# A squared-ReLU attention and GeGLU block: transposing DMAs by row chunk, stores as operations of their own, loads spread out, and the first batch in two query halves

## The chip, the cores and the metric

The kernel runs on one core of one Trainium2 chip. The metric is the device time of one execution in microseconds, the median of several runs.

## The reference

For 8 batches, 12 heads, 448 positions and a head width of 64, attention with a squared ReLU in place of a softmax; the heads are then laid side by side to rows of 768, and a gated feed-forward block with 1536 hidden columns follows:

```python
scores = scale * np.matmul(q, k.transpose(0, 1, 3, 2))     # scale = 1/8
attn = np.maximum(scores, 0.0) ** 2 / S
x = np.matmul(attn, v)            # to (B * S, H * D) = (3584, 768)
g = x @ w_gate
gelu = 0.5 * g * (1.0 + erf(g * inv_sqrt2))
out = gelu * (x @ w_val) @ w_out  # (3584, 768), float32
```

All inputs are float32; the kernel computes in bfloat16 and accumulates in float32.

## The kernel before

**Tiles.** TensorE is used as four 64x64 quarters. Every matmul (line 151, `mm`) names its row half and its column half; rows 0 and rows 1 are planned as two streams, PE0 and PE1. Positions are dealt so that partition p holds positions 7p to 7p+6 (`SC` = 7 chunks of `P` = 64).

**Work of a batch.** There are 21 score units (`add_scores`): each is a block of transposed scores, 128 x 896, of which ScalarE makes the ReLU (`rl`, line 339) and VectorE the square (`attnT`, line 345). `add_values` multiplies them with v for a pair of heads and VectorE scales the result into `xT` (line 394). When all six pairs are there, `add_gate_value` computes the 12 column blocks `fc` of gate (g = 0) and value (g = 1), 6 contraction steps each; ScalarE makes the gelu, VectorE the product, `uT`. `add_out` computes one tile of 128 rows in two column halves, ScalarE copies it to `osb` (line 484), and SP stores it (line 489).

**q and k must be transposed** (tile `qkT`) for the scores. For batches 0 to 2 (`EARLY` = 3) TensorE does it (`add_transposes`, line 290) with VectorE copying the result (line 296). For batches 3 to 7 `add_dma_transposes` does it: VectorE reorders q and k into `qkr` in seven copies (line 240), and one transposing DMA, issued by SP, writes all of `qkT` (line 248).

**Order.** `work` is a list of due times: attention of batch b+1 is spread under gates, values and outputs of batch b; batch 0's attention stands ahead of everything. `run_plan` then places all operations on a model clock. PE0 and GpSimd keep the given order; PE1, ScalarE, VectorE and SP take from a pool what is ready first. The result is one fixed order per engine, and each engine runs its order without overtaking. PSUM has two buffers for scores (`SB`) and a ring of four for everything else (`FB`): a ring buffer is free when VectorE or ScalarE has emptied it.

**Loads** are all issued by GpSimd in one order, and land in it: batch 0 in head groups, then the weight chunks `wg`/`wv` 0 to 5 with batch 1's heads between them, the four `wo` chunks, and then what `add_gate_value` adds as it goes: batch 2 as a whole (q, k, v), later batches in three parts per tensor, q and k three batches ahead and v two. A tile's two buffers (`qkv` pool) are reused every second batch.

**Stores** are issued inside the emission of ScalarE's copy of the second column half. They stand in SP's order at the place where that copy was planned; SP's order also holds the transposing DMAs.

Of the kernel before, what the change touches and what calls it, by code (L numbers as in the profile page):

```python
# [85 lines left out]
def kernel(  # L86
# [17 lines left out]
    P = 64  # L104
# [15 lines left out]
    EARLY = 3  # L120
# [13 lines left out]
    opool = ctx.enter_context(tc.tile_pool(name="opool", bufs=3))  # L134
# [95 lines left out]
    def add_dma_transposes(b):  # L230

        box = {}

        wait = Op("IDLE", 8.0, lambda: None, [head_op[b, pr, i] for pr in range(NPAIR) for i in range(2)])
        IDLE.append(wait)

        def emit_copy(c):
            if not box:
                box[0] = lpool.tile([128, SC, H, D], bf16, name="qkr", tag="qkr")
            nc.vector.tensor_copy(  # L240
                box[0][:, c], qk16[b].rearrange("p (h c d) -> p c h d", c=SC, d=D)[:, c])

        copies = [Op("DVE", 0.4, lambda c=c: emit_copy(c),
                     [wait, tr_op.get(b - 1)], lag=0.1, prio=3)
                  for c in range(SC)]
        DVE.extend(copies)
        r_op[b] = copies
        tr_op[b] = Op("SP", 7.0, lambda: nc.sync.dma_start_transpose(
            qkT_tile(b)[:, :, :], box[0].rearrange("p c h d -> p (c h d)")),
            [*copies, last_s.get(b - 2)], lag=6.0)  # L250
        SP.append(tr_op[b])
# [10 lines left out]
    def both(at, ops):  # L262

        for lo, hi in ops:
            lower.append((at, lo))
            pairs.append(("with", lo, hi))
# [13 lines left out]
    def add_transposes(at, b, m):  # L280
# [30 lines left out]
        both(at, zip(*ops))  # L311

    def add_scores(at, b, u):


        m, w = divmod(u, SC)
        tail = w == VC - 1
        prs = (2 * m, 2 * m + 1) if tail else (2 * m + (w > VC - 1),)
        cl = w if w < VC else w - VC
        box = {}  # L320

        def emit(j, pr):
            if not box:
                box[0] = psS.tile([128, 2, 512], f32, name="sp", tag="S")
            sp = box[0]
            t = qkT_tile(b).rearrange("d (c r) x -> d r c x", c=SC)[HALF[j], pr]
            for i in range(2):
                if tail:
                    n0 = (pr % 2) * S // 2
                    qs = t[:, :, i * P // 2:(i + 1) * P // 2]  # L330
                    mm(sp[HALF[i], j, n0:n0 + S // 2].rearrange("k (c p) -> k c p", c=SC),
                       t[:, VC - 1, HALF[1]], qs, j, i, True, True)
                else:
                    mm(sp[HALF[i], j, 0:S].rearrange("k (c p) -> k c p", c=SC),
                       t[:, cl + i * VC, HALF[1]], t[:, :, HALF[0]], j, i, True, True)

        def emit_relu():
            rl = box[1] = rpool.tile([128, 2, S], bf16, name="rl", tag="rl")
            nc.scalar.activation(rl[:, :, :], box[0][:, :, 0:S], AF.Relu)  # L339

        def emit_sq():
            a = apool.tile([128, 2, S], bf16, name="attnT", tag="attnT")
            for pr in prs:
                att[b, pr, VC - 1 if tail else cl] = a
            nc.vector.tensor_tensor(a[:, :, :], box[1][:, :, :], box[1][:, :, :], op=ALU.mult)  # L345

        if b < EARLY:
            have = [t_op[b, m, 0], t_op[b, m, 1]]
        else:
            have = [tr_op[b]]  # L350
        have = [*have, *units[-SB:1 - SB]]
        ops = [[Op(f"PE{j}", 0.095 if tail else 0.189, lambda j=j, pr=pr: emit(j, pr), have, lag=0.24)
                for pr in prs] for j in range(2)]
        last_s[b] = ops[1][-1]
        relu = Op("ACT", 0.92, emit_relu, [ops[0][-1], ops[1][-1], *sq_list[-4:-3]], lag=0.06, prio=2)
        n_a = len(sq_list)
        sq = Op("DVE", 0.64, emit_sq, [relu, *att_free[n_a - 12:n_a - 11]] if n_a >= 12 else [relu],
                lag=0.1, prio=2)
        units.append(relu)
        sq_list.append(sq)  # L360
        att_free.append(None)
        for pr in prs:
            sq_op.setdefault((b, pr), []).append((sq, n_a))
        ACT.append(relu)
        DVE.append(sq)
        both(at, zip(*ops))
# [3 lines left out]
    def add_values(at, b, pr):  # L370
        box = {}

        def emit(i, w):
            if pr == 0 and i == 0 and w == 0:
                xT[b] = xpool.tile([128, KC, S], bf16, name="xT", tag="xT")
            if not box:
                box[0] = psF.tile([128, 512], f32, name="ff", tag="F")
            if i == 1 and w == VC - 1:
                wait_lower(box)
            for j in range(2):  # L380
                o = box[0][HALF[j], 0:S]
                a = att[b, pr, w][HALF[i], j, :]
                if w < VC - 1:
                    ins = mm(o, v16[b][HALF[i], 2 * pr + j, w + i, :], a, i, j,
                       i == 0 and w == 0, i == 1 and w == VC - 2)
                else:
                    ins = mm(o.rearrange("d (c p) -> d c p", c=SC)[:, :, i * P // 2:(i + 1) * P // 2],
                       v16[b][HALF[i], 2 * pr + j, (1 - i) * (VC - 1), :],
                       a[:, (pr % 2) * S // 2:(pr % 2 + 1) * S // 2].rearrange(
                           "k (c p) -> k c p", c=SC), i, j, False, False)  # L390
            box[1] = ins

        def emit_copy():
            nc.vector.tensor_scalar_mul(xT[b][:, pr, :], box[0][:, 0:S], scalar1=out_scale)  # L394

        sqs = sq_op[b, pr]
        have = [*(s for s, _ in sqs), head_op[b, pr, 2], head_op[b, pr, 3]]
        order = ([0, 1, 2, 3], [3, 0, 1, 2])
        ops = [[Op(f"PE{i}", 0.189 if w < VC - 1 else 0.095, lambda i=i, w=w: emit(i, w),
# [5 lines left out]
        x_op[b, pr] = Op("DVE", 0.63, emit_copy, [o_op[b, pr]], lag=0.1, prio=1)  # L405
        DVE.append(x_op[b, pr])
        ring.append(x_op[b, pr])
        then(at, 0.0, *ops, x_op[b, pr])
# [5 lines left out]
    def add_gate_value(at, b, fc, g):  # L414

        i, o = divmod(fc * 128, WCH)
# [3 lines left out]
        def emit(r, dc):  # L420
# [4 lines left out]
            for j in range(2):  # L425
                ins = mm(box[0][HALF[j], 0:S], w[HALF[r], dc, o + P * j:o + P * (j + 1)],
                         xT[b][HALF[r], dc, :], r, j, r == 0 and dc == 0, r == 1 and dc == KC - 1)
            box[1] = ins

        def emit_gelu():  # L430
            gel[b, fc] = gpool.tile([128, S], bf16, name="gel", tag="gel")
            nc.scalar.activation(gel[b, fc][:, :], box[0][:, 0:S], AF.Gelu)  # L432

        def emit_mult():
            if fc == 0:
                uT[b] = upool.tile([128, FC, S], bf16, name="uT", tag="uT")
            nc.vector.tensor_tensor(uT[b][:, fc, :], gel.pop((b, fc))[:, :],  # L437
                                    box[0][:, 0:S], op=ALU.mult)

        ops = [[Op(f"PE{r}", GS, lambda r=r, dc=dc: emit(r, dc),  # L440
                   [w12_op[i][g], x_op[b, dc], *(ring_dep() if r == 0 and dc == 0 else ())], lag=0.24)
                for dc in range(KC)] for r in range(2)]
        if g == 0:
            done = gel_op[b, fc] = Op("ACT", 0.55, emit_gelu, [ops[1][-1]], lag=0.06, prio=0)
            ACT.append(done)
        else:
            done = u_op[b, fc] = Op("DVE", 0.63, emit_mult, [gel_op[b, fc], ops[1][-1]],
                                    lag=0.1, prio=0)
            DVE.append(done)
            if EARLY <= b + 2 < B and fc == 0:  # L450
                add_dma_transposes(b + 2)
            if b == 0 and fc == 0:
                load_heads(2, 0, H)
            elif b + 2 < B and b and 6 <= fc < 9:
                load_v(b + 2, 4 * (fc - 6), 4 * (fc - 5), [done])
            if b + 3 < B and fc < 6:
                h0 = 4 * (fc % 3)
                load_qk(b + 3, fc // 3, h0, h0 + 4, [done])
        ring.append(done)
        then(at, GS, *ops, done)  # L460

    def add_out(at, t, g):
# [17 lines left out]
        def emit_copy():  # L480
# [4 lines left out]
            if g < NG - 1:  # L485
                return
            for j, (b, c) in enumerate(chunks):
                rows = out[b * S:(b + 1) * S, :].rearrange("(p c) d -> c p d", c=SC)
                nc.sync.dma_start(rows[c], ob[HALF[j], :])  # L489

        ops = [[Op(f"PE{r}", RS, lambda r=r, fc=fc: emit(r, fc),
                   [wo_op[fc // WOG], *(u_op[b, fc] for b, _ in chunks),
# [4 lines left out]
        ACT.append(cp)  # L497
        then(at, RS, *ops, cp)
# [5 lines left out]
    load_heads(1, 0, 4)  # L504
    load_w12(1)
    load_w12(2)
    load_heads(1, 4, 8)
    load_w12(3)
    load_heads(1, 8, 12)
    load_w12(4)  # L510
    load_w12(5)
    for i in range(FC // WOG):
        load_wo(i)

# [6 lines left out]
    for b in range(B):  # L521
        starts.append(at)
        for fc in range(FC):
# [11 lines left out]
    for b in range(B):  # L535
        if b == 0:
            lo, hi = -60.0, -12.0
        elif b == 1:
            lo, hi = -8.0, starts[1] - LEAD
# [6 lines left out]
        for pr in range(NPAIR):  # L546
            u = SC * (pr // 2) + (VC - 1, SC - 1)[pr % 2]
            work.append((lo + u * step + max(4.5, (3.2 if b == 0 else 2.5) * step), 2, add_values, (b, pr)))
# [5 lines left out]
    for at, _, fn, args in work:  # L554
        fn(at, *args)
# [75 lines left out]
```

## Time and profile before

| | us |
|---|---|
| runs | 454.03, 455.63, 452.81 (median 454.03) |
| profiled execution, whole time | 456.05 |
| its span in the profile | 454.2 |

The page divides the span into 40 slices of 11.4 us, gives each engine's busy time, the chain of work that ended last, and groups of instructions by line: engine, what it writes and reads, shapes, count, then busy time, mean ns of one, and the engine's idle time before them with what ended it. Some groups around the change:

```profile
L339 ACT ACTIVATE rl<-sp 128x896 bf16<-128x896 f32 x168 | 152.6, 920 | 119.7 <-PE sp L151 102.2
...
L432 ACT ACTIVATE gel<-ff 128x448 bf16<-128x448 f32 x96 | 52.2, 544 | 57.4 <-PE ff L151 55.8
...
L290 PE MATMUL ff<-ident,qk 64*64 64x64 bf16 x504 | 15.2, 213 | 7.4 <-DMA qk<-in_q_dram 3.3
```

The DMA issues (what, queue, count, size of one, median time from issue to landing):

```profile
wv<-in_moe_w_val_dram POOLq DMA_DIRECT2D x6, 384.0 KB, 11.3
wo<-in_moe_w_out_dram POOLq DMA_DIRECT2D x4, 576.0 KB, 15.7
v<-in_v_dram POOLq DMA_DIRECT2D x2, 384.0 KB, 22.0
```

Sizes are of the bfloat16 side; HBM is read in float32.

### The profile page before, as it was taken

The page shows a single profiled execution, that of the slowest core. Times are in us where ns is not written, and L with a number is a line of the kernel's source. Part 1 is how long each engine was busy: PE and PEld are TensorE (multiplying, and loading weights), DVE is VectorE, ACT ScalarE, POOL GpSimd, SP SyncE. Part 2 cuts the span into 40 slices and gives each one's busy share as a digit, 9 for nine tenths or more (in the row PEclk, how much of TensorE's full clock was granted, in tenths as well). Part 3 has the DMA queues.
Part 4 walks back from the last instruction along what each step waited for, and adds up shares of the span by engine and source line. Part 5 has one row for each costly group of instructions (what it writes and reads, how often), then busy time and mean ns, then how long its engine had stood idle before and what let it go on. Part 6 is the DMA issues. An engine that isn't in the chain of part 4 may idle for free.

```text
span 454.2 us, 20046 instructions
## 1 busy us (share of the span) xinstructions
PE 429.1 (94%) x9360; PEld 364.6 (80%) x9360; DVE 207.7 (46%) x366; ACT 226.0 (50%) x322; POOL 70.7 (16%) x114
## 2 busy tenths in 40 slices
PE   5779999999799999999999799999999999999995
PEld 2546987878699778987799578999999878987895
DVE  1794555464453356545553255535543355312200
ACT  1785554545355555555555455555555655422121
POOL 9545421041301500060002000030000000000000
PEclk8595999999999999999999899999999999999998
DMA  7999999389938960497009800291002200120024
GB/s 100 187 198 198 204 208 202 74 107 156 162 55 136 222 100 3 81 197 146 3 3 153 183 1 3 57 207 39 3 3 73 72 4 3 38 73 3 3 72 105
DMA packets 68659, 43.56 MB, mean 96 GB/s; under 512 B 29664, under 2 KB 64992, under 8 KB 68576
## 3 DMA queue, kind: packets, MB, share of 16 engines
q0 software_dynamic: 37056, 24.39, 37.9%
q1 hardware_dynamic: 31520, 17.90, 18.7%
q8 instruction: 73, 1.20, 1.1%
q14 instruction: 10, 0.08, 0.0%
HBM read 48.76 MB, written 11.01 MB: 132 GB/s over the span
## 4 chain that ended last, share of the span: by engine, by line
PE 87%; DMA 4%; ACT 3%; POOL 2%; issue 2%; DVE 2%; SPq 0%; ACTq 0%; POOLq 0%
PE ff L151 78%; PE sp L151 8%; DMA out_dram<-osb 2%; ACT rl L339 2%; DMA qk<-in_k_dram 2%; PE ff L290 1%; POOL qk L198 1%; POOL v L211 1%; DVE qkT L296 1%; DVE attnT L345 1%; ACT osb L484 0%; SPq L489 0%; DVE xT L394 0%; DVE uT L437 0%; POOL ident masks.py:199 0%
## 5 line engine op out<-in xcount | busy, mean ns | idle before, releaser
L151 PE MATMUL ff<-xT,wg 64*64 64x448 bf16 x2304 | 230.5, 353 | 4.0 <-ACT osb L484 3.3
L151 PE MATMUL ff<-xT,wv 64*64 64x448 bf16 x2304 | 229.7, 351 | 0.4 <-issue 0.4
L339 ACT ACTIVATE rl<-sp 128x896 bf16<-128x896 f32 x168 | 152.6, 920 | 119.7 <-PE sp L151 102.2
L151 PEld LDWEIGHTS <-wg 64*64 64x64 bf16 x2304 | 133.4, 108 | 25.6 <-issue 8.4
L151 PE MATMUL ff<-wo,uT 64*64 64x384 bf16 x2688 | 149.9, 323 | 0.3 <-DVE uT L437 0.2
L151 PEld LDWEIGHTS <-wv 64*64 64x64 bf16 x2304 | 134.0, 108 | 18.1 <-issue 2.2
L345 DVE TENSOR_TENSOR attnT<-rl 128x896 bf16<-128x896 bf16 x168 | 104.0, 623 | 92.2 <-ACT rl L339 91.4
L151 PEld LDWEIGHTS <-uT 64*64 64x64 bf16 x2688 | 124.4, 107 | 5.8 <-DVE uT L437 0.6
L151 PE MATMUL sp<-qkT 64*64 64x448 bf16 (+1 forms) x768 | 115.7, 350 | 7.0 <-ACT rl L339 4.3
L437 DVE TENSOR_TENSOR uT<-gel,ff 128x448 bf16<-128x448 bf16 x96 | 59.5, 620 | 75.8 <-PE ff L151 71.3
L151 PE MATMUL ff<-attnT,v 64*64 64x448 bf16 (+1 forms) x768 | 91.6, 339 | 0.0
L432 ACT ACTIVATE gel<-ff 128x448 bf16<-128x448 f32 x96 | 52.2, 544 | 57.4 <-PE ff L151 55.8
L151 PEld LDWEIGHTS <-qkT 64*64 64x64 bf16 x768 | 48.1, 112 | 20.1 <-issue 11.5
L211 POOL DMA_DIRECT2D v<-in_v_dram x46 | 28.8, 649 | 166.1 <-PE sp L151 87.8
L151 PEld LDWEIGHTS <-v 64*64 64x64 bf16 x768 | 48.4, 110 | 3.8 <-issue 0.3
L484 ACT COPY osb<-ff 128x384 f32<-128x384 f32 x56 | 26.8, 479 | 46.1 <-PE ff L151 37.4
L394 DVE TENSOR_SCALAR xT<-ff 128x448 bf16<-128x448 f32 x48 | 29.9, 624 | 39.2 <-PE ff L151 33.4
L290 PE MATMUL ff<-ident,qk 64*64 64x64 bf16 x504 | 15.2, 213 | 7.4 <-DMA qk<-in_q_dram 3.3
L198 POOL DMA_DIRECT2D qk<-in_q_dram x23 | 14.8, 653 | 41.0 <-DVE qkr L240 21.3
L290 PEld LDWEIGHTS <-qk 64*64 64x64 bf16 x504 | 14.3, 127 | 8.1 <-DMA qk<-in_q_dram 3.8
L296 DVE COPY qkT<-ff 128x896 bf16<-128x896 bf16 x18 | 10.9, 623 | 14.3 <-PE ff L290 12.1
L198 POOL DMA_DIRECT2D qk<-in_k_dram x23 | 14.6, 644 | 14.4 <-DMA qk<-in_k_dram 4.3
(17 smaller groups left out, 33.3 us busy)
## 6 DMA issues: line engine op xcount, KB each, us to landing
out_dram<-osb SPq DMA_DIRECT2D x56, 192.0 KB, 4.0
v<-in_v_dram POOLq DMA_DIRECT2D x40, 128.0 KB, 7.1
qk<-in_q_dram POOLq DMA_DIRECT2D x20, 224.0 KB, 9.8
qk<-in_k_dram POOLq DMA_DIRECT2D x20, 224.0 KB, 10.8
wg<-in_moe_w_gate_dram POOLq DMA_DIRECT2D x6, 384.0 KB, 11.0
wv<-in_moe_w_val_dram POOLq DMA_DIRECT2D x6, 384.0 KB, 11.3
wo<-in_moe_w_out_dram POOLq DMA_DIRECT2D x4, 576.0 KB, 15.7
v<-in_v_dram POOLq DMA_DIRECT2D x2, 384.0 KB, 22.0
```

The source lines that it names most:

```text
L151: return nc.tensor.matmul(o, lhsT, rhs, start=start, stop=stop, tile_position=(P * row, P * col))
L198: op = load(4 * (h1 - h0) * S * D, lambda: nc.gpsimd.dma_start(tile_of().rearrange("p (h x) -> p h x", h=H)[:, h0:h1, :], src[b, h0:h1].re ...
L211: nc.gpsimd.dma_start(v16[b][HALF[i], h0:h1, :, :], v[b, h0:h1].rearrange("h (p c) d -> p h c d", c=SC)[:, :, c0:c0 + VC, :])
L290: nc.tensor.transpose(t[HALF[j], pr, c * P:(c + 1) * P], src[HALF[i], 2 * (2 * m + pr) + j, c, :], ident[HALF[i], HALF[i]], tile_position= ...
L296: nc.vector.tensor_copy(dst[:, 2 * m:2 * m + 2, :, HALF[i]], box[i].rearrange("d r (c p) -> d r c p", c=SC))
L339: nc.scalar.activation(rl[:, :, :], box[0][:, :, 0:S], AF.Relu)
L345: nc.vector.tensor_tensor(a[:, :, :], box[1][:, :, :], box[1][:, :, :], op=ALU.mult)
L394: nc.vector.tensor_scalar_mul(xT[b][:, pr, :], box[0][:, 0:S], scalar1=out_scale)
L432: nc.scalar.activation(gel[b, fc][:, :], box[0][:, 0:S], AF.Gelu)
L437: nc.vector.tensor_tensor(uT[b][:, fc, :], gel.pop((b, fc))[:, :], box[0][:, 0:S], op=ALU.mult)
L484: nc.scalar.copy(ob[:, cols], box[0][:, 0:OGS])
```

## The change

- `EARLY` is 2: batch 2 is transposed by DMA too. Its `add_dma_transposes` is called just before its first score unit is added.
- The transposing DMA of a batch is seven DMAs, one per row chunk c, each behind its own `qkr` copy. Scores of the batch depend on all seven.
- The planned wait between the landing of q and k and the copies is 2 us instead of 8.
- Each store is an operation of its own in SP's pool, with the lowest priority number; `osb` has four buffers instead of three.
- Loads: chunks 1 and 2 of `wg`/`wv` stand before batch 1's heads, q and k of batch 2 before `wo`, v of batch 2 after it. From batch 3 on, q and k are loaded two batches ahead instead of three: one part behind each of the first six products of batch b, then v behind the next three.
- Batch 0 is worked through in two halves `hq` of its queries (32 of the 64 positions of each chunk): score units of 448, 448, 448 and 224 columns per two pairs, values, and gates and values of the first `NA` = 6 column blocks, all at half width. Scores of the second half are due from 6 us ahead of the first gates on. Blocks 6 to 11 are computed at full width.
- Batch 1's attention is due from 5.0 instead of -8.0; a few planned costs are written as formulas of the width.

```diff
-    EARLY = 3
+    NA = 6
+    EARLY = 2
...
-    opool = ctx.enter_context(tc.tile_pool(name="opool", bufs=3))
+    opool = ctx.enter_context(tc.tile_pool(name="opool", bufs=4))
...
-        wait = Op("IDLE", 8.0, lambda: None, [head_op[b, pr, i] for pr in range(NPAIR) for i in range(2)])
+        wait = Op("IDLE", 2.0, lambda: None, [head_op[b, pr, i] for pr in range(NPAIR) for i in range(2)])
...
-        tr_op[b] = Op("SP", 7.0, lambda: nc.sync.dma_start_transpose(
-            qkT_tile(b)[:, :, :], box[0].rearrange("p c h d -> p (c h d)")),
-            [*copies, last_s.get(b - 2)], lag=6.0)
-        SP.append(tr_op[b])
+        tr_op[b] = [Op("SP", 1.1, lambda c=c: nc.sync.dma_start_transpose(
+            qkT_tile(b).rearrange("d (c r) x -> d c r x", c=SC)[:, c],
+            box[0][:, c].rearrange("p h d -> p (h d)")),
+            [copies[c], last_s.get(b - 2)], lag=6.0) for c in range(SC)]
+        SP.extend(tr_op[b])
...
+    def pieces(b, u):
+        m, w = divmod(u, SC if b else 2 * 4)
+        x, y = 2 * m, 2 * m + 1
+        mid = VC - 1
+        if b:
...
+        n = S // 4
+        return [[(x, 0, 0, 2 * n), (x, 1, 2 * n, 2 * n)],
+                [(x, 2, 0, 2 * n), (x, mid, 2 * n, n), (y, mid, 3 * n, n)],
+                [(y, 0, 0, 2 * n), (y, 1, 2 * n, 2 * n)],
+                [(y, 2, 0, 2 * n)]][w % 4]
...
-            have = [tr_op[b]]
+            have = tr_op[b]
...
-    def add_gate_value(at, b, fc, g):
+    def add_gate_value(at, b, fc, g, hq=None):
+        p0, QP = (0, P) if hq is None else (hq * P // 2, P // 2)
+        N = SC * QP
...
-            if EARLY <= b + 2 < B and fc == 0:
-                add_dma_transposes(b + 2)
-            if b == 0 and fc == 0:
-                load_heads(2, 0, H)
-            elif b + 2 < B and b and 6 <= fc < 9:
-                load_v(b + 2, 4 * (fc - 6), 4 * (fc - 5), [done])
-            if b + 3 < B and fc < 6:
+            if b + 2 < B and b and fc < 9:
                 h0 = 4 * (fc % 3)
-                load_qk(b + 3, fc // 3, h0, h0 + 4, [done])
+                if fc < 6:
+                    load_qk(b + 2, fc // 3, h0, h0 + 4, [done])
+                else:
+                    load_v(b + 2, h0, h0 + 4, [done])
+                if fc == 5:
+                    add_dma_transposes(b + 2)
...
-            if g < NG - 1:
-                return
-            for j, (b, c) in enumerate(chunks):
-                rows = out[b * S:(b + 1) * S, :].rearrange("(p c) d -> c p d", c=SC)
-                nc.sync.dma_start(rows[c], ob[HALF[j], :])
+        def emit_store(j):
+            b, c = chunks[j]
+            rows = out[b * S:(b + 1) * S, :].rearrange("(p c) d -> c p d", c=SC)
+            nc.sync.dma_start(rows[c], osb[t][HALF[j], :])
...
+        if g == NG - 1:
+            SP.extend(Op("SP", 0.6, lambda j=j: emit_store(j), [cp], prio=-1) for j in range(2))
...
     load_w12(0)
-    load_heads(1, 0, 4)
     load_w12(1)
     load_w12(2)
+    load_heads(1, 0, 4)
+    load_w12(3)
     load_heads(1, 4, 8)
-    load_w12(3)
+    load_w12(4)
     load_heads(1, 8, 12)
-    load_w12(4)
     load_w12(5)
+    load_qk(2, 0, 0, H)
+    load_qk(2, 1, 0, H)
     for i in range(FC // WOG):
         load_wo(i)
+    load_v(2, 0, H)
...
+        for hq in range(0 if b else 2):
+            for fc in range(NA):
+                for g in range(2):
+                    work.append((at, 5, add_gate_value, (b, fc, g, hq)))
+                    at += G / 2
+        for fc in range(0 if b else NA, FC):
...
+    for hq in range(2):
+        lo, step = ((-60, 2.0), (-6.0, 0.9))[hq]
+        for u in range(4 * NPAIR // 2):
+            work.append((lo + u * step, 3, add_scores, (0, u, hq)))
```

## The prediction

> **What bounds the kernel now.** I read the page from the top: which engine is busy, at what clock, in which slices.
>
> ```profile
> PE 429.1 (94%) x9360; PEld 364.6 (80%) x9360; DVE 207.7 (46%) x366; ACT 226.0 (50%) x322; POOL 70.7 (16%) x114
> ...
> PE   5779999999799999999999799999999999999995
> ...
> PEclk8595999999999999999999899999999999999998
> DMA  7999999389938960497009800291002200120024
> ```
>
> TensorE is the bound, except at the start: its clock is down in the first four slices, while the DMA row is full. "Busy" says little here, since a matmul that uses a quarter of the array counts as busy. So I count work. In the windows 410 to 420 us (220 matmuls of 64x448) and 430 to 440 us (254 of 64x384) TensorE is packed: 0.102 ns for each streamed column, edges included. I take 0.104, so a 448-column matmul is 47 ns of work. The page's counts give (4608 + 672 + 672) x 448 + 2688 x 384 + 504 x 64 columns (the scores and values, 768 each, count as 672, a quarter of them being half wide): 388.6 us of work. The other 65.6 us of the 454.2 us span are lost. Counting the same way by window, the loss is 31.8 us before 50 us, 3.5 to 80, 8.4 to 130, 4.5 to 250, 4.4 in 250 to 260, 6.4 to 440 and 6.4 in the tail.
>
> The windows show the three kinds of loss:
>
> ```profile
> 25.00:50.00 25.00, 21.64 (x392) 16.15 (x392) 16.68 (x29) 16.45 (x21) 13.15 (x19) 0.80 1.42 198
> ...
> 110.00:120.00 10.00, 7.11 (x174) 5.17 (x174) 4.28 (x8) 3.08 (x6) 1.31 (x3) 1.00 1.35 166
> ...
> 250.00:260.00 10.00, 7.42 (x130) 4.88 (x125) 2.21 (x4) 4.63 (x7) 0.08 (x1) 0.83 0.89 204
> ```
>
> Columns: length, busy time and count of TensorE, weight loads, VectorE, ScalarE, GpSimd, clock, DMA. Where a packed window of 10 us has 220 matmuls, 250 to 260 has 130, and part of it at half clock. The chain of waits names the causes (start, length, what), and the SP queue's timeline shows what stands behind the second:
>
> ```profile
> 115.20 2.54 issue
> ...
> 246.53 6.21 DMA out_dram<-osb
> ```
> ```profile
> 94.97 50.58 SPq L248 DMA_TRANSPOSE qkT<-qkr  x2
> ...
> 238.84 7.01 SPq L248 DMA_TRANSPOSE qkT<-qkr  x1
> 245.94 10.05 SPq L489 DMA_DIRECT2D out_dram<-osb  x8
> ```
>
> Stores wait in SP's queue behind one transposing DMA of 7 us. ScalarE's copy then waits 4.0 us for a free `osb`, TensorE 2.6 us for ScalarE.
>
> The DMA view settles my forecast; first 104 to 108 us, where the transposing DMA of batch 3 meets loads, then 140 to 144 us, where one runs alone:
>
> ```profile
> q0 software_dynamic: 713, 0.57, 89.8%
> q1 hardware_dynamic: 712, 0.18, 34.6%
> ...
> qkT<-qkr SPq DMA_TRANSPOSE x1, 27.3
> ```
> ```profile
> q1 hardware_dynamic: 3134, 0.80, 147.9%
> ...
> qkT<-qkr SPq DMA_TRANSPOSE x1, 8.7
> ```
>
> Packets go one for one. A transpose is 5376 packets of 256 bytes, 336 for each of 16 engines: 6.9 us alone. Beside loads it gets one packet per load packet, and took 27.3 us to land instead of 8.7.
>
> [...]
>
> **The change, part by part.** Positions are work issued before an instruction, in the order in which the built program issues.
>
> *First batch in halves.* The first gate matmul moves from 10.3 us of work (reached at 37.6 us) to 6.7. Its ScalarE chain: 10.5 relu units per half at 0.82 us back to back (nine in 7.40 us); the heads land as before (the last q and k near 17 us). About 18 relu units stand before the first gelu, so gates begin near 28 us. The next block is batch 1's first transposes at 9.2 us of work. With two more gate/value chunks loaded ahead of them (four loads, 2.0 us apart in the trace), these heads land at about 33.7 us (25.7 in the trace). Before stood at 9.2 at 34 us too, but still had its first gates to wait for and ran at half clock through the page's fourth slice (34 to 45 us)[...]. I take it to be 3 us of work ahead at 50 us. Cost: 312 more matmuls net. [...] VectorE and ScalarE get 15 and 9 more, shorter, instructions; both are idle half the time. All this lies ahead of the wait named next, which hides it; uncovered it would be 0 to 3 us.
>
> *Loads moved.* q and k of batch 2 (672 KB each) go ahead of the four `wo` loads, v of batch 2 behind. The last `wv` lands at 53.7 us (issued 42.36, median 11.3); q and k took 3.35 us each (k is 3.3 us behind q). So k of batch 2 lands at 60.4 us. VectorE, in order, now has a `qkr` copy of batch 2 at 26 us of work, waiting for that k: behind it stand gate multiplies, hence PSUM banks, so TensorE is at 30 or less at 60.4 us (before: 27.4). Whatever the halves win beyond that is lost here.
>
> *Batch 2 by DMA.* 168 TensorE transposes go: 1.1 us of work, and the loss around them. Each window of ten us with 56 of them loses about 1.5 us more than its neighbours; 112 lie after the place below. In their stead seven `qkr` copies (0.354 us each, VectorE has room) and seven transposing DMAs. The four stores of batch 0 stand behind them on SP, which is no loss: they come later anyway. The DMAs start at 61 to 66 us, with `wo` and v of batch 2 (192 packets per engine, to 76.2 us without company) in flight. One for one, 192 of the 336 go by while the loads last; the rest follow. If nothing is lost in sharing, all is done at 76.2 + 6.9 + 1 = 84. In the one meeting that the trace has (the same 192 load packets, 10.8 us alone), loads plus transpose took 23.3 us, so the transpose added 12.5: 76.2 + 12.5 + 1 = 90. I take 87.5. The first score matmul of batch 2 waits for all seven and stands at 44.2 us of work. TensorE would be there at 60.6 + 14.2/0.94 = 76 us (`wo`, delayed by 96 transpose packets, is in by 76). So it waits some 11 us, everything behind it in its one order too: outputs of batch 0, gates of batch 1. Before passed 44.2 at 79.4. [...]
>
> *Stores and transposes later.* Seven short issues in place of one of 7 us, stores on their own, a fourth `osb`: the loss in 250 to 260 us (4.2 above the base), 150 to 160 (1.4) and 300 to 310 (1.0) goes. Could it cost? Each store still waits in line behind transposes, but those stand a third of a batch earlier, 13 us of work ahead of their use against 9.8 us of landing. Next in line would be that margin. Loads of q and k one per gate column, not two batches ahead: 4 to 5 us to landing against about 5 us in the order; a late one stops VectorE for a microsecond. I add 1.5 us for both (0 to 4).
>
> **Sum.** Remaining work at the wait is 387.5 - 44.2 = 343.3 us, 7.7 of it in the last 14.2 us, which stay. The rest runs with the loss that 130 to 250 and 260 to 440 us show without the store waits, (10.9 - 2.4) in 300 us, 2.8%: 345.2. So 87.5 + 2.6 + 345.2 + 14.2 + 1.5 = 451.0 of span, against 454.2: 3.2 less. The profiled execution took 456.05 in all, 1.85 beyond its span; the median is 454.03. I forecast 454.0 - 3.2 = 451 (rounded), and 447 to 455 for 84 to 91 us. Less than 1% (4.5 us) I count as no change that a measurement of this kernel can tell.
>
> **Rivals.** *The transpose isn't late*: sharing is cheaper, or the wait shorter than I see. TensorE passes 44.2 at 76 to 83 us: 436 to 446, faster. For: the alternating packets at 104 to 108 us add up without loss. Against: the 27.3 us. *The transpose is very late*: at 100 to 104 us the two queues crept. If the sharing goes that way throughout, at 80 ns per transpose packet, 192 of them put the loads' end to 92 and the rest to 96: 460, slower. It is slower than before from a landing at about 91 us, by over 1% from 95. *The store waits stay*: SP still takes its queue in order; then 6.6 us come back: 456 to 458.
>
> **Chances.** Forecast mechanism 0.60, transpose in time 0.18, very late 0.12, store waits stay 0.10. Faster by over 1%: 0.18 and nearly 0.4 of the first, 0.41. Slower: 0.12 and a little of the last, 0.13. Same: 0.46. The range 439 to 458 leaves out half of the second case and most of the third.
>
> **What would show it.** Right: gates from about 28 us; transposing DMAs issued at 61 to 66 us and the last landing at 84 to 91; TensorE idle at the first `sp` matmul of batch 2 with the DMA as its releaser, and half clock after; no wait of ScalarE on `out_dram` in the middle. Wrong: no idle time between 75 and 90 us, a landing outside 84 to 91, or a wait in each batch on `qkr` copies or transposes.

## The result, and the profile after

| | before | after |
|---|---|---|
| runs | 454.03, 455.63, 452.81, 455.41 | 460.44, 460.9, 461.96, 458.95 |
| median | 454.72 | 460.67 |
| profiled execution, whole time | 456.05 | 460.44 |
| its span | 454.2 | 458.7 |

The ratio is 1.0134 (95% interval 1.0085 to 1.0183): slower, by about 6 us, where 3 less were forecast. (Medians and ratios here are taken over undisturbed runs alone, and a ratio can differ a little from the quotient of two medians.)

The page of the kernel after, busy shares and rows of 40 slices (11.5 us each):

```profile
PE 430.5 (94%) x9672; PEld 382.4 (83%) x9672; DVE 207.5 (45%) x382; ACT 226.7 (49%) x331; POOL 70.7 (15%) x114
...
PE   6896579879999999999999999999999999999995
...
PEclk8559899979999999999999999999999999999998
DMA  8999999929635490729374881762092200120023
```

After slice 9 little is lost. The damage is in slices 4 to 9, where the row of before had 9s: TensorE at 6, 5, 7 tenths with the DMA row at 9. The chain of waits of after (start, length, what) names it; these are all its lines over 1.4 us between 35 and 95 us that are no work of TensorE:

```profile
39.22 2.41 issue
...
45.39 2.43 issue
...
51.34 2.69 issue
...
58.48 1.46 issue
...
63.95 1.92 issue
...
88.60 5.93 DMA qkT<-qkr
```

Two things, then. Five gaps of about 2 us, one every 6 us, that no semaphore explains ("issue"). And the wait on the transposes of batch 2, forecast for 76 to 87.5 us. The chain counts it from the issue of the last transposing DMA; TensorE itself waits less, as its own waits between 75 and 100 us show (what, on what: total us, times, longest):

```profile
PE sp L152 <- DMA qkT<-qkr: 3.0, 1, 3.0
PE ff L152 <- issue: 1.7, 1, 1.7
```

It stands at 88.7 to 90.4 us in a sixth gap, works for 1.3 us, and waits for the transposes from 91.7 to 94.7.

The same counting of work as in the prediction (0.104 ns per column) gives, over time, what TensorE had done in after less what it had done in before:

| at us | 45 | 50 | 55 | 60 | 70 | 85 | 95 | 105 | 250 | 270 | 430 |
|---|---|---|---|---|---|---|---|---|---|---|---|
| us of work | +1.6 | -1.1 | -4.5 | -6.5 | -10.7 | -8.6 | -13.5 | -15.5 | -10.4 | -6.2 | -5.2 |

At 70 us after is 10.7 us behind. Seven more go between 85 and 105: at the sixth gap, at the transposes and in the half clock behind them (94.3 to 101.1 us). Some 10 come back: 4 between 105 and 120 us, where before has a stall of its own, and 4 at 250 to 270, where the store waits are gone.

**The five gaps.** The windows of 38 to 68 us, in before and in after (length; busy and count of TensorE, weight loads, VectorE, ScalarE, GpSimd; clock; DMA share, over 1 where packets overlap in time; GB/s):

```profile
38.00:68.00 30.00, 29.88 (x634) 26.52 (x632) 16.71 (x29) 16.27 (x22) 11.59 (x16) 0.89 1.30 204
```
```profile
38.00:68.00 30.00, 19.18 (x600) 17.06 (x599) 11.33 (x25) 11.73 (x19) 9.55 (x13) 0.93 1.30 204
```

Look at the counts. Before executes 634 matmuls in these 30 us and after 600: nearly the same number, but after's are narrow, so it needs only 19 us for them and stands still for 11. So the limit counts instructions, not columns (e1 below). Numbering all instructions of TensorE (a weight load and a matmul each count one), the gaps stand at number 1473, 1729, 1985, 2241 and 2497: exactly 256 apart. The sixth, at 3521, is on the same grid. The DMA view of after, 38 to 68 us, has a queue that the prediction passed over (packets, MB, share):

```profile
q0 software_dynamic: 7817, 6.01, 128.9%
q8 instruction: 5, 0.08, 1.0%
```

Five packets of 16384 bytes, at 39.19, 45.55, 51.58, 57.66 and 63.53 us; each of the five gaps ends 2.3 to 2.5 us after one of them starts. In the whole execution the queue has 75 such packets; at 256 instructions each that is 19200, and TensorE executes 19344. In before it has 73, which makes 18688, and TensorE executes 18720. So I take them to be TensorE's own instructions, 256 to a packet. In the load phase, then, TensorE gets 256 instructions per 6.1 us: 128 pairs of weight load and matmul, 48 ns a pair. A 448-column matmul is 47 ns of work, so a stream of them just fits. A narrower one costs as much as a full one there (in e1 below, 264 more cost some 12 us, 45 ns each).

**The transposes.** The timeline of SP's queue in after, then the DMA view of 82 to 92 us:

```profile
73.43 18.58 SPq L249 DMA_TRANSPOSE qkT<-qkr  x7
```
```profile
q0 software_dynamic: 1185, 0.99, 76.5%
q1 hardware_dynamic: 1665, 0.41, 61.3%
...
qkT<-qkr SPq DMA_TRANSPOSE x3, 11.6
```

They are issued at 73.4 to 88.6 us, not 61 to 66. The copies stand in VectorE's order behind gate products, which are late (73.0 to 80.1 us); and the seventh DMA is issued 6.3 us behind the sixth, long after its copy. The loads they meet are not `wo` and v alone: the q and k loads of batch 3, issued by GpSimd at 77.5 to 80.7 us, land at 82.8 to 92.9:

```profile
77.54 1.94 POOL L199 DMA_DIRECT2D qk<-in_q_dram  x3 [22.92 <-PE ff L292]
```

The diff puts those loads behind the gate products of batch 1 (`[done]`), but that is an order for the planner: the first of these products comes at 111.2 us. On the chip GpSimd has nothing to do in between and waits for the free `qk` buffer only, that is, for TensorE's transposes of batch 1 (L292).

### The profile page after: what moved, and what is told of

The parts are those of the page before. It is cut to its first block, busy times and chain, and to the rows that moved or that the text cites. A ratio compares the mean times of both kernels' runs of the same rounds, so it can differ in the third digit from the quotient of the medians.

```text
span 458.7 us, 20811 instructions
## 1 busy us (share of the span) xinstructions
PE 430.5 (94%) x9672; PEld 382.4 (83%) x9672; DVE 207.5 (45%) x382; ACT 226.7 (49%) x331; POOL 70.7 (15%) x114
## 4 chain that ended last, share of the span: by engine, by line
PE 90%; issue 3%; DMA 3%; ACT 2%; POOL 1%; DVE 1%; POOLq 0%; ACTq 0%
PE ff L152 81%; PE sp L152 8%; ACT rl L360 1%; DMA qkT<-qkr 1%; DMA qk<-in_k_dram 1%; PE ff L292 1%; POOL qk L199 1%; POOL v L212 1%; DVE qkT L298 1%; ACT osb L515 0%; DVE xT L417 0%; POOL ident masks.py:199 0%; POOL ident masks.py:197 0%; POOLq masks.py:199 0%; ACTq L360 0%
## 5 line engine op out<-in xcount | busy, mean ns | idle before, releaser
L152 PE MATMUL ff<-xT,wv 64*64 64x448 bf16 (+1 forms) x2448 | 226.2, 342 | 5.1 <-issue 5.1
L152 PE MATMUL ff<-xT,wg 64*64 64x448 bf16 (+1 forms) x2448 | 227.0, 343 | 2.4 <-issue 2.4
L360 ACT ACTIVATE rl<-sp 128x896 bf16<-128x896 f32 (+1 forms) x171 | 153.2, 904 | 138.1 <-PE sp L152 106.2
L152 PEld LDWEIGHTS <-wg 64*64 64x64 bf16 x2448 | 138.5, 109 | 15.5 <-issue 2.9
L366 DVE TENSOR_TENSOR attnT<-rl 128x896 bf16<-128x896 bf16 (+1 forms) x171 | 104.6, 614 | 90.5 <-ACT rl L360 89.4
L152 PE MATMUL sp<-qkT 64*64 64x448 bf16 (+2 forms) x864 | 116.4, 334 | 7.8 <-DMA qkT<-qkr 3.0
L152 PE MATMUL ff<-attnT,v 64*64 64x448 bf16 (+2 forms) x864 | 97.9, 333 | 2.0 <-issue 1.9
L466 DVE TENSOR_TENSOR uT<-gel,ff 128x448 bf16<-128x448 bf16 (+1 forms) x102 | 60.4, 592 | 85.2 <-PE ff L152 82.7
L461 ACT ACTIVATE gel<-ff 128x448 bf16<-128x448 f32 (+1 forms) x102 | 53.1, 521 | 53.7 <-PE ff L152 52.8
L417 DVE TENSOR_SCALAR xT<-ff 128x448 bf16<-128x448 f32 (+1 forms) x54 | 30.9, 572 | 39.6 <-PE ff L152 36.7
L241 DVE COPY qkr<-qk 128x768 bf16<-128x768 bf16 x42 | 13.5, 354 | 0.0
L292 PE MATMUL ff<-ident,qk 64*64 64x64 bf16 x336 | 10.4, 209 | 2.9 <-DMA qk<-in_q_dram 1.8
L292 PEld LDWEIGHTS <-qk 64*64 64x64 bf16 x336 | 9.1, 123 | 4.7 <-DMA qk<-in_q_dram 1.9
## 6 DMA issues: line engine op xcount, KB each, us to landing
wv<-in_moe_w_val_dram POOLq DMA_DIRECT2D x6, 384.0 KB, 11.6
```

Source lines behind the costliest of these rows:

```text
L152: return nc.tensor.matmul(o, lhsT, rhs, start=start, stop=stop, tile_position=(P * row, P * col))
L241: nc.vector.tensor_copy(box[0][:, c], qk16[b].rearrange("p (h c d) -> p c h d", c=SC, d=D)[:, c])
L292: nc.tensor.transpose(t[HALF[j], pr, c * P:(c + 1) * P], src[HALF[i], 2 * (2 * m + pr) + j, c, :], ident[HALF[i], HALF[i]], tile_position= ...
L360: nc.scalar.activation(rl[:, :, 0:W], box[0][:, :, 0:W], AF.Relu)
L366: nc.vector.tensor_tensor(a[:, :, 0:W], box[1][:, :, 0:W], box[1][:, :, 0:W], op=ALU.mult)
L417: nc.vector.tensor_scalar_mul(half_of(xT[b][:, pr, :], hq * QP, QP), box[0][:, 0:N].rearrange("d (c p) -> d c p", c=SC), scalar1=out_scale)
```

## Experiments

Times are medians; "work" is counted as above, against before. Where the expectations of e1 to e4 name theories by letters, A is the supply of instructions to TensorE, B that a narrow matmul costs its own execution alone, and C that the transposes land late whenever they are issued.

**e1, e2: the narrow matmuls alone.** In the kernel before, the gate and value matmuls of column blocks 0 to 5 of one batch are cut in two, 264 more matmuls. e1 cuts batch 0, in the load phase; e2 cuts batch 5.

```diff
-            for j in range(2):
-                ins = mm(box[0][HALF[j], 0:S], w[HALF[r], dc, o + P * j:o + P * (j + 1)],
-                         xT[b][HALF[r], dc, :], r, j, r == 0 and dc == 0, r == 1 and dc == KC - 1)
+            cut = [slice(0, S // 2), slice(S // 2, S)] if b == 0 and fc < 6 and r + dc else [slice(0, S)]
+            for cs in cut:
+                for j in range(2):
+                    ins = mm(box[0][HALF[j], cs], w[HALF[r], dc, o + P * j:o + P * (j + 1)],
+                             xT[b][HALF[r], dc, cs], r, j, r == 0 and dc == 0,
+                             r == 1 and dc == KC - 1 and cs is cut[-1])
```

> The kernel before with 264 of the gate and value matmuls of batch 0's column blocks 0 to 5 each cut in two of 224 columns: same order, same work, 528 more TensorE instructions. Theory A (while loads fill the DMA engines, TensorE gets 256 instructions per some 6 us, so more instructions cost time even where the columns stay): two more blocks of 256, 8 to 13 us longer, with idle stretches of 2 to 3 us that nothing in the profile explains, 256 instructions apart. Theory B [...]: at most 1 us longer.

Measured: 467.04, ratio 1.0259 (1.0184 to 1.0335), some 12 us more. Chain of waits of e1, its waits of TensorE between 45 and 70 us:

```profile
48.36 2.21 issue
...
54.31 2.18 issue
...
60.09 2.32 issue
...
67.37 1.24 issue
```

At instructions 1473, 1729, 1985 and 2241, the very numbers of after, in a kernel without halved attention and without the new transposes; 671 matmuls in 38 to 68 us. At 70 us it is 9.7 us of work behind.

> The same cut in batch 5, where the DMA engines are mostly idle. Theory A: instructions arrive in time, 0 to 3 us longer, no idle stretches. If instructions are short at any time: as long as the cut in batch 0, 8 to 13 us. Theory B: at most 1 us.

Measured: 459.87, ratio 1.0121 (1.0085 to 1.0157). The same 264 matmuls, the same columns, here cost less than half. Windows of e2 around them:

```profile
300.00:310.00 10.00, 8.38 (x284) 7.92 (x279) 3.74 (x6) 4.04 (x6) 0.33 (x1) 1.00 0.75 147
310.00:320.00 10.00, 9.88 (x356) 9.61 (x348) 4.88 (x9) 5.44 (x8) 0.00 (x0) 1.00 0.02 5
```

From 310 us on the DMA share is 0.02, and TensorE executes 356 matmuls in 10 us, where after had 200; instruction packets come every 3.5 us (its weight loads and matmuls, 704 in the 10 us, are 256 per 3.6 us). The only gap in these windows (303.64, 1.62 us, at number 12481, on the same grid) falls where transfers still run. The trace has about 2 us lost there; the medians say 4.4 and the ratio 5.5, more than the 0 to 3 that I had expected, so that size stays open. What follows from the two: most of what narrow matmuls cost in the load phase they cost because of when they run.

**e3: gates of batch 0 at full width** (attention still halved; its second half due earlier).

```diff
-    NA = 6
+    NA = 0
...
-        lo, step = ((-60, 2.0), (-6.0, 0.9))[hq]
+        lo, step = ((-60, 2.0), (-18.0, 0.9))[hq]
```

> The changed kernel with NA = 0: attention of batch 0 still in two halves (the second due 12 us earlier), but all its gates and values at full width: 576 TensorE instructions fewer in the load phase. Theory A: 2 blocks of 256 fewer, so batch 2's transposing DMAs are issued at 61 to 68 us, not 73 to 89, and land at 84 to 90; 450 to 455 us. Theory C (the transposing DMAs are late because they share the engines with loads, whenever TensorE gets there): landing near 94 us again, 458 to 461.

Measured: 458.08, ratio 1.0058 (1.0037 to 1.0079). The longest gap on the grid before 75 us is 1.1 us; at 65 us it is only 0.9 us behind before. The copies come at 61.7 to 69.1, and the SP timeline of e3 shows the DMAs issued from 62 us on, as I had forecast:

```profile
62.13 27.28 SPq L249 DMA_TRANSPOSE qkT<-qkr  x7
```

But their issue drags on to 86.7, they land at 93.3, one us before those of after, and TensorE stands from 81.9 to 93.5. Starting eleven us earlier bought one, as theory C has it. Between lie the loads of batch 3, issued at 67.2 to 76.3.

**e5: after, with those loads held** until batch 2 is turned: the first q load of batch 3 waits for a transposing DMA of batch 2.

```diff
...
+            if b == 3 and (i, h0) == (0, 0):
+                tc.add_manual_dep(ins.ins, turned[2].ins.name, SYNC, reason="hold")
...
```

> The changed kernel, with the first q load of batch 3 (and so every load behind it on GpSimd's queue) held until the last of three of batch 2's seven transposing DMAs is done. Nothing else moves. Theory: the transposes of batch 2 land at 94.5 us because they share the engines one for one with the q and k loads of batch 3, which the plan put behind products but which on the chip wait only for a free buffer. Held back, those loads leave the engines to the transposes, which are issued at 73 to 89 us as before (the copies set that) and land about 1 to 2 us after each issue; TensorE comes to the first scores of batch 2 at 88.7 us and waits 0 to 3 us, with at most one window of half clock: 451 to 455. Rival (the transposes are slow by themselves, or the seventh, issued at 88.6 us, is late because of its copy): the last still lands at 91 us or later, and the time stays within 2 us of the changed kernel's 460.7.

Measured: 452.47, ratio 0.996 (0.9938 to 0.9981), 8 us less than after. In the trace the wait is for the last of the seven. The SP timeline of e5:

```profile
73.10 12.06 SPq L256 DMA_TRANSPOSE qkT<-qkr  x7
```

Issued from 73.1 as in after, but the seven take 12.1 us there instead of 18.6, close behind their copies, and the last lands at 86.7 instead of 94.5. TensorE comes to the first scores of batch 2 near 90 us, does not wait, and keeps its full clock (granted 1.00 from 80 to 150 us, where after has 0.72 from 90 to 100). The gaps of the load phase remain (8.9 us of work behind at 85 us). So of after's loss the wait, the sixth gap and the half clock are the work of the loads of batch 3.

**e6: e3 and the hold together.**

> The same hold, and gates and values of batch 0 at full width (NA = 0, its attention still in two halves). Theory: without the narrow matmuls the copies are ready at 62 to 70 us, so the transposes now share the engines only with wo and v of batch 2, as my prediction assumed: the last lands at 80 to 88 us. TensorE is at the first scores of batch 2 at about 82 us, waits 0 to 6 us: 448 to 454. Rival (landing is set by something other than the loads of batch 3): landing near 92 us again, 458 as with NA = 0 alone.

Measured: 450.23, ratio 0.9898 (0.9844 to 0.9953). This is the company that the prediction described: only `wo` and v beside them, last landing at 86.4. The copies come at 61.5 to 69.1, yet the DMAs are issued at 61.9 to 82.5. TensorE's wait in e6:

```profile
PE sp L152 <- DMA qkT<-qkr: 3.1, 1, 3.1
```

Then comes half clock for 3.4 us (86.9 to 90.3). Beside e5, the narrow matmuls cost only 2.2 us here: the wait hides the rest.

**e4, e7, e8: each half of the change alone.** e4 has batch 0 at full width and batch 2 transposed by TensorE, with before's load order; what stays of the change are the seven short transposing DMAs for batches 3 to 7 with the shorter planned wait, the stores as own operations, the fourth `osb`, and q and k two batches ahead. e7 is after with `EARLY = 3`; e8 is after with batch 0 at full width.

```diff
-    EARLY = 2
+    EARLY = 3
...
-        if fn is add_scores and args == (2, 0):
-            add_dma_transposes(2)
```
```diff
-    NA = 6
+    NA = 0
...
-        m, w = divmod(u, SC if b else 2 * 4)
+        m, w = divmod(u, SC)
...
-            lo, hi = 5.0, starts[1] - LEAD
+            lo, hi = -8.0, starts[1] - LEAD
```

The first diff is e7 whole, the second the core of e8 (the due times of batch 0 are before's as well); e4 has both, with the calls of the initial loads as in before.

> The changed kernel with batch 0 at full width, batch 2 transposed on TensorE and the load order of before: what is left is the seven transposing DMAs per batch 3 to 7, stores as operations of their own, the fourth osb, and q and k two batches ahead. By my sum for the later part: the store waits go, 6 to 8 us shorter than before, 446 to 449. If those parts do nothing: 454 to 456.

Measured: 449.09, ratio 0.987 (0.9817 to 0.9923), better than both kernels. No wait on `out_dram`, and no half clock between 43 and 446 us. Counted as work, 3 us come back between 105 and 120 us, where before has a stall at 115, and 4 between 250 and 270.

> The changed kernel with batch 2 transposed on TensorE again (EARLY = 3) and the load order as the change has it; batch 0 still in two query halves. Theory: what the narrow matmuls lose while instructions come slowly (about 10 us at 70 us, less 3 to 6 us that the transposes' wait cost otherwise) stays, the wait at 88.7 us goes: gaps of about 2 us at every 256th instruction between 39 and 64 us remain, no wait on a transposing DMA before 130 us: 454 to 459. Rival (the halves cost nothing, the transposes of batch 2 are all of the loss): 449 as with full width.

Measured: 459.65, ratio 1.0107 (1.0059 to 1.0155), just above what was expected. No wait on a transposing DMA before 130 us, and the gaps are there (2.16 us at 46.17, 2.78 at 57.67 the longest): 9.8 us behind before at 105 us, where e4 is 1.9 behind. Halving costs some 10 us where no wait hides it; but e4 and e7 differ in the load order and in the due times of batch 1 too, so that not all of it is shown to be the halves.

> The changed kernel with batch 0 at full width throughout; batch 2 still by transposing DMA, loads as the change has them. Theory: no gaps at every 256th instruction, the copies are ready early, but the transposes land only when the loads of batch 3 run dry, near 88 to 93 us; TensorE waits 6 to 11 us for them: 453 to 458. Rival (the narrow matmuls are all of the loss): 449.

Measured: 458.14, ratio 1.0078 (1.0047 to 1.011). The transposes are issued at 65.1 to 87.0 and land at 92.2. The waits of TensorE in e8 (what, on what: total us, times, longest):

```profile
PE sp L152 <- DMA qkT<-qkr: 11.0, 1, 11.0
```

So the halves add 10.6 us to e4, the transposing DMAs of batch 2 with the new loads 9.1, and both together 11.6 (460.67). They don't add up, by 8 us, since both end at one place: TensorE waits 11.0 us for the transposes in e8, and in after, which comes there later by its gaps, only 3.0.

**e12: batch 2 by DMA at its best:** e8 with the hold of e5.

> Batch 0 at full width, batch 2 by transposing DMA, loads as the change has them, and the q and k loads of batch 3 held until the last transpose of batch 2 is done. Theory: copies are ready at 65 to 81 us, the transposes share with wo and v of batch 2 alone and land at 83 to 87 us instead of 92; TensorE is there at about 81 us and waits 3 to 6 us, with one window of half clock: 449 to 452, so that batch 2 by DMA gains nothing on e4 even without the loads. Rival (with the loads away the transposes land before TensorE comes, at 81 us or earlier): 444 to 447, better than e4.

Measured: 450.61, ratio 0.9932 (0.9908 to 0.9956). Last landing at 84.0, and TensorE waits 4.3 us for it; batch 2 by DMA gains nothing on TensorE's own transposes even with the loads of batch 3 out of the way.

**e9, e10, e11: which part ends the store waits.** e9 is before with one buffer more. e10 is e4 with one less. e11 is e4 again.

```diff
-    opool = ctx.enter_context(tc.tile_pool(name="opool", bufs=3))
+    opool = ctx.enter_context(tc.tile_pool(name="opool", bufs=4))
```

> The kernel before with one more output buffer: osb has four instead of three, nothing else. Theory: the wait of ScalarE on out_dram at 246.5 us (6.2 us in the chain of waits) is a matter of buffers: with a fourth, the stores that stand behind the 7 us transposing DMA on SP no longer hold ScalarE, and the 4 to 6 us of work lost between 250 and 260 us come back: 449 to 451. Rival (one buffer more is not enough, since eight stores stand behind that DMA, and it needs the shorter issues on SP as well): at most 2 us gained, a wait on out_dram remains in the middle of the trace.

Measured: 452.05 over 13 runs (448.13 to 454.41), ratio 0.9983 (0.9946 to 1.002). The window of e9 that held 130 matmuls and a clock of 0.83 in before:

```profile
250.00:260.00 10.00, 10.00 (x217) 9.23 (x209) 4.09 (x7) 6.08 (x10) 1.73 (x3) 1.00 1.07 221
```

The wait is gone, as the theory has it; 4.3 us of work come back between 250 and 270. But the medians show 2.1 us, which the interval doesn't tell from nothing, and the 449 to 451 expected did not come. The stall that before has at 115 us is still there (116.28, 2.53 us), and in the profiled execution some 2 us went to 3.4 us of half clock behind it (120.4 to 123.8), which before's profile did not have. Whether that takes the rest in the other runs isn't shown: inconclusive for the time.

> The version with batch 0 at full width and batch 2 transposed on TensorE (e4), with osb back at three buffers: seven short transposing DMAs per batch and stores as operations of their own, but not the fourth buffer. Theory (short issues and own stores are enough): no wait on out_dram between 240 and 270 us, 449 as e4. Rival (the fourth buffer does it): a wait of 2 to 6 us on out_dram there again, 451 to 455.

Measured: 449.66, ratio 0.99 (0.9865 to 0.9936); no wait on `out_dram`. Short issues and own stores are enough without the fourth buffer.

> The version of e4 once more, in more rounds and beside the other candidates: 448.5 to 450, ratio 0.985 to 0.992.

Measured: 449.73, ratio 0.9896 (0.9865 to 0.9928). It is the best version found, with e10 level.

## Why the prediction was wrong

The sum put the end of the wait at 87.5 and the rest at 363.5 (2.6 for half clock behind the wait, then 345.2 + 14.2 + 1.5). The trace has 94.6 and 364.1. So 7.1 of the 7.7 us by which the span was missed lie ahead of the first scores of batch 2. (The work of before is 388.0 us by the formula of the prediction, not 388.6; nothing hangs on it.) Step by step:

- **"First batch in halves": the step that failed first.** Gates begin at 29.5 us (28 was said), and TensorE is ahead by 1.6 us at 45. But "3 us of work ahead at 50 us" is -1.1, and by 70 us it is 10.7 us behind. I priced the narrow matmuls by their execution at full supply, and that was an estimate: before's trace gives 25 ns for a transpose of 64 columns (84 in 2.1 us busy, 40 to 60 us), and what a stream of 224 or 112 columns takes I had not measured. What was short is instructions: 256 per 6.1 us while the loads run (e1 shows it with nothing else changed, e2 that most of it passes with the loads). "Uncovered it would be 0 to 3 us" was some 10 in e7. That the wait behind hides the cost was right for the most part: full-width gates alone take 2.6 us off after (e3).
- **"Loads moved" held:** k of batch 2 lands at 60.2 (60.4). "VectorE has a copy waiting for that k" did not: the copies stand behind gate products in VectorE's order, and came with them, late, at 73 us.
- **"Batch 2 by DMA": the step that moved the time, since the partner was wrong.** Sharing with `wo` and v alone, the landing was put at 84 to 90. After shares with the q and k loads of batch 3 as well, since I read their dependency on gate products as a wait on the chip, and lands at 94.5. Of lateness and company, the company decides: early issue with those loads lands at 93.3 (e3), late issue without them at 86.7 (e5), early issue without them at 86.4 (e6). Holding the loads takes 8.2 us off after and brings it to 452.47, where 451 was forecast. Issue "at 61 to 66" was 73 to 89. That is not the lateness alone: with the copies in time, e6 still issues at 61.9 to 82.5. TensorE, said to be there at 76 us, stops at 81.9 in e3, 83.5 in e6 and 91.7 in after, so that the 11 us of wait were 3.0.
- **The half clock after it** was put at a cost of 2.6 us, which was my estimate. It was 6.8 us long (94.3 to 101.1, granted clock 0.50), a loss of 3.4: right but for 0.8 us. It followed on waits of 1.7 and 3.0 us. In before, 3.4 us of half clock (253.0 to 256.4, again 0.50) follow on the wait of 2.6 us. What sets its length no run here shows.
- **"Stores and transposes later" held.** The window of 250 to 260 us loses 0.1 us, no ScalarE wait on `out_dram` is left, and the late part came out within 0.6 us. "q and k in about 5 us in the order" was wrong in the same way as above, without harm in the later batches: these loads come early, not late.

Of the rivals, "very late" has the right time (460, landing 92 to 96) and the wrong reason: the transposes shared not badly but with more loads, and began 12 us late. That its time came out is luck. Its chance was too small because the company of the transposes was taken as settled. The range ended at 458 for the same reason.

## What to carry to other kernels

Before cutting matmuls finer, count instructions: see in the DMA view how often a packet of TensorE's instructions arrives in that stretch (here 256 of them per 6.1 us), and compare with what the narrower stream would use up. A dependency in a planner orders a plan; ask of every moved load what its issuing engine really waits for, and what it will meet on the DMA engines if it goes early. Two delays that end at the same wait cost little more than the larger one (10.6 and 9.1 us here, 11.6 together), so repair both before judging either.

## What the hardware showed that I had not expected

- TensorE's instructions come by DMA, 16384 bytes and 256 instructions at a time as far as the packets and the gaps tell, and with the engines full of loads (share 1.30) one such packet per 6.1 us was all that came in after. With few transfers the spacing fell to 3.5 us in e2 (310 to 320 us), without a gap. Where the 6 us go, in waiting behind load packets or in a late request, no run here shows.
- The stall at 115.2 us of before, 2.54 us of "issue", is at instruction 4289, on the same grid of 256, while a transposing DMA and loads run. Gates at full width are no protection there: e6 has two such gaps, 1.4 us at 68.7 and 1.7 at 76.3, with packets 7.2 to 7.5 us apart while its transposing DMAs run beside the loads. e4 and e5 have none at 4289. The prediction quoted that line and did not ask what it was.
- Seven short transposing DMAs are not issued in one go: in e6, with the copies there by 69.4 us, the fourth to the sixth took 2.4 to 3.9 us each to issue; in e5, with few loads about, 1.3 us. What holds them, no run here shows.
